# A chain of sigmoid attention and two gated products: layers three and four in four quarters of one form, with a single ScalarE function

## The chip, the core and the metric

The kernel runs on one core of a Trainium2 chip. The metric is device time in microseconds (us), the median of three runs. One further execution was profiled; all rows below come from it.

## The reference, cut to what matters

Four blocks of 448 tokens go through a sigmoid attention (not touched here) and four layers, all in fp32:

```python
x = attention(q, k, v)                                    # 1792 tokens x 768
h = np.maximum(np.maximum(x @ w1, x @ w2), x @ w3)        # layer one, 768 x 768 each
z = h @ moe_w_out                                         # layer two, 768 x 768
h = z @ moe2_w_in                                         # layer three, 768 x 2048
g = h * (1.0 / (1.0 + np.exp(-1.702 * h)))                # the nonlinearity
out = g @ moe2_w_out                                      # layer four, 2048 x 768
```

## The kernel before

**Numbers.** TensorE multiplies in a rounded fp32 format (fp32r). For accuracy every operand is split into a high half (a cast) and a low half (the operand minus its cast), and each product is three matmuls: high by high, high by low, low by high. A cast can go on ScalarE or VectorE (`copy`, L310), a difference only on VectorE (`two`, L313).

**Seven products for eight.** Layers one to three are computed by Strassen's scheme in Winograd's form on blocks of 2 x 2. `moving` makes the seven moving operands from the four blocks of a layer's input (differences, then a high and a low half each, in pieces of 2 x 448 and 448 columns). `Weights` makes the seven stationary operands of a pair of weight tiles: four sums of 128x384 and seven splits, or loads the finished ones from memory (`kept`). A `Set` is one pair of weight tiles over two token blocks: seven products of nine matmuls (L493), and then additions from PSUM that give four tiles of 128x448.

**Layers three and four.** The 1,792 tokens are two pairs of blocks, tp = 1 and tp = 0, and the 2,048 hidden features are 16 tiles, which layer three takes as eight pairs, fp = 0 to 7. A `Group` is one pair for one tp. It runs its Set of layer three; the tiles go through a sigmoid on ScalarE (L828), a multiply and a split on VectorE. Layer four follows directly: `unit` i multiplies the weights of the two feature tiles with the split tiles, six matmuls (L866 to L868), and adds the result on VectorE to the output so far; three of the twelve units keep their PSUM bank from group to group instead. The units of a group are interleaved with the products of the next group's Set. In this way run fp 0 to 3 of tp = 1, then all eight of tp = 0. What is left, fp 4 to 7 of tp = 1, is the last quarter and has a form of its own: its four Sets are staggered by `stage`, and then layer four over all four pairs is done by seven products as well (`Four` splits a moving operand of 4 x 448 columns, `operand4` a weight operand of 128x1536, `combine` and `wide` make the combinations, `product4` at L1008 issues twelve matmuls for each third of the outputs, `finish` adds the first half's result, which was kept in memory as `spill`, and stores). Weights of layer four were split once, kept in memory (`kept4`) and loaded again. The input of layer three is loaded from memory (`reload`) and split again when tp changes.

**The order.** Nothing here is issued as it is written. Each operation is recorded with what it reads and writes, a duration estimate and a due time, and `Order.run` plays the program through once: a free engine takes the ready operation that is due first. The result is a fixed order for each engine, and on the chip each engine goes through its own in that order. `soon` sets a due time a little ahead: with it the conversions of raw 64-bit weights to fp32 (`single`: two instructions on ScalarE, L358 and L363, three on VectorE, one of them L373) are strewn between other work. `prepare` and `prepare4` convert and store a tile for later. All DMAs are issued by one queue, SyncE's.

Of the kernel before, what the change touches and what calls it, by code (L numbers as in the profile page):

```python
# [7 lines left out]
F32 = mybir.dt.float32  # L8
# [178 lines left out]
T = S  # L187
# [6 lines left out]
MW = 15 * T  # L194
NW = 15 * T
FW = 17344
# [7 lines left out]
REDO = (1, 3, 5, 7)  # L204


def moe_chain_kernel(tc, qk, vv, wa, wb, out):
# [20 lines left out]
    sn1, s2, sn2 = Space(NW), Space(MW, gate=lambda: gate["m"]), Space(NW, gate=lambda: gate["n"])  # L228
    sn3, sn4 = Space(8 * T, gate=lambda: gate["n3"]), Space(NW - 8 * T, gate=lambda: gate["n3"])
# [6 lines left out]

    def to_n2(e):
        npool[0].release()
        npool[0] = pool("n2", side="right")
        slab_n.append(npool[0].tile([P, NW], F32R, name="n2"))  # L240
# [7 lines left out]
    def F(at, n):  # L248
        if at >= FAR2:
            return Reg(sn4, at - FAR2, n, lambda: slab_n[3][:, at - FAR2 : at - FAR2 + n])  # L250
# [7 lines left out]
    def R(at, n):  # L258
        if at >= FAR2:
            return Reg(sn3, at - FAR2, n, lambda: slab_n[2][:, at - FAR2 : at - FAR2 + n])  # L260
        if at >= FAR:
            return Reg(sn2, at - FAR, n, lambda: slab_n[1][:, at - FAR : at - FAR + n])
        if at >= RW:
            return Reg(s2, at - RW, n, lambda: slab_m[1][:, at - RW : at - RW + n])
        return Reg(sr, at, n, lambda: slab_r[:, at : at + n])

# [61 lines left out]
    assert y0 + 4 * DM == FW  # L328
# [54 lines left out]
    def split(hi, lo, x, n):  # L383
        copy(hi, x, n)
        sub(lo, x, hi, n)
# [409 lines left out]
    gate["n"] = O.op({"-": 0.0}, to_n2, after=set(sn1.ops))  # L795

    zslots = [slots[i] for i in (1, 2, 3, 4, 5, 6, 0)]
    s3 = 12 * T  # L800
    b3, b4 = Round(range(3)), Round(range(3, 5))
    stay = {2: 5, 6: 6, 10: 7}
    g_at = Round([RW, FAR])
    w4_at = Round([RW + 8 * T + OFF, FAR + 8 * T + OFF, RW + 8 * T + OFF + 2 * DM, FAR + 8 * T + OFF + 2 * DM])
    temp_at.places += [12 * T + 2 * DM + i * T for i in range(2)]
    assert 12 * T + 2 * DM + 2 * T <= tv and 8 * T + OFF + 4 * DM <= min(MW, NW)
    PAIRS = NF // 2

    class Group:


        def __init__(self, fp, tp, z):
            self.fp, self.tp, self.g, self.w = fp, tp, {}, None
            first = self.first = (tp == 1) == (fp < PAIRS // 2)
            early = self.early = fp < EARLY or fp >= PAIRS // 2
            self.set = Set(z, lambda: Weights(12 + fp, first and fp >= READY, s3, early), self.put, b3)
            self.at = None

        def put(self, half, tok, ps, other):
            if self.at is None:  # L820
                self.at = g_at()
            at = self.at + (4 * half + 2 * tok) * T
            if other is not None:
                new = temp()
                add(new, ps, other, S)
                ps = new
# [5 lines left out]
            self.g[half, tok] = hi, lo  # L832

        def weights(self):
            self.w = []
            for half in range(2):
                f, at = self.fp + 8 * half, w4_at()
                hi, lo, both = R(at, DM), R(at + DM, DM), R(at, 2 * DM)
                if self.first:
                    y = F(y_at(), DM)  # L840
                    if self.early:
                        dma(y, y4[f], 384)
                    else:
                        single(wb[tile4(f)], y, "ACT")
                    split(hi, lo, y, DM)
                    if self.fp < PAIRS // 2:
                        dma(kept4[f], both, 768)
                else:
                    dma(both, kept4[f], 768)
                self.w.append((hi, lo))  # L850

        def unit(self, i):
            if self.w is None:
                self.weights()
            tok, o = 1 - i // KC, i % KC
            b = 2 * self.tp + tok
            stays = i in stay
            fresh = not stays or self.fp == 0
            ps, c = banks(stay[i] if stays else b4()), slice(o * P, (o + 1) * P)
            w, g = self.w, [self.g[half, tok] for half in range(2)]  # L860

            def f(_):
                for j in range(2):
                    wh, wl, gh, gl = w[j][0](), w[j][1](), g[j][0](), g[j][1]()
# [275 lines left out]
```

## Time and profile before

| | |
|---|---|
| median of three runs | 866.35 us (865.92 to 868.24) |
| the profiled execution | 865.97 us, its span 864.1 us |
| TensorE (PE) busy | 858.4 us, 99% |
| VectorE (DVE) busy | 684.2 us, 79% |
| ScalarE (ACT) busy | 508.2 us, 59% |
| granted TensorE clock | 1.000 of full speed throughout |
| moved by DMA | 238 MB, mean 276 GB/s |

The span is the time from the first to the last instruction of the program; the execution's time holds some 1.9 us besides. TensorE has two rows in a profile: PE is the matmuls, PEld the weight loads in front of them, which run beside the matmul before. The end of a matmul's record is modelled and reaches past the start of the next, so the rate is read from start to start. The stages of the program follow each other on TensorE: attention to 131.9 us, layers one and two to 434.3, layers three and four to 860.4.

### The profile page before, as it was taken

What the parts mean: (1) busy time and instruction counts of PE and PEld (TensorE: products, weight loads), DVE (VectorE), ACT (ScalarE), POOL (GpSimd) and SP (SyncE); (2) the same over time, 40 slices, a digit from 0 to 9 for tenths busy, and PEclk for the clock granted to TensorE, in tenths of its full rate; (3) what the DMA queues carried; (4) which work ended last, traced back from release to release, by engine and by line L of the source; (5) the groups of instructions that cost most, each with busy time, mean ns of one, the idle gap of its engine ahead of it and who ended that gap; (6) DMA issues with size and microseconds to landing.
All of it is one profiled execution on the core that took longest, in us unless ns stands there. A gap on an engine that the chain in (4) does not pass through costs nothing.

```text
span 864.1 us, 12626 instructions
## 1 busy us (share of the span) xinstructions
PE 858.4 (99%) x4555; PEld 747.8 (87%) x4555; DVE 684.2 (79%) x1096; ACT 508.2 (59%) x743; POOL 0.3 (0%) x5
## 2 busy tenths in 40 slices
PE   9999999999999999999999999999999999999998
PEld 5544548999999999999989999999999999999997
DVE  5898898888898788888597887756696888753894
ACT  7899898565466556667365345655665434423540
POOL 0000000000000000000000000000000000000000
PEclk9999999999999999999999999999999999999999
DMA  8898976877649997899979847988878674786123
GB/s 316 282 369 318 380 264 221 325 243 250 224 170 395 359 378 284 324 333 362 403 295 344 310 144 239 404 317 354 292 237 319 220 258 154 231 281 196 32 64 129
DMA packets 77534, 238.14 MB, mean 276 GB/s; under 512 B 8608, under 2 KB 18208, under 8 KB 77472
## 3 DMA queue, kind: packets, MB, share of 16 engines
q1 hardware_dynamic: 77472, 237.34, 76.7%
q8 instruction: 36, 0.59, 0.3%
q14 instruction: 26, 0.21, 0.1%
HBM read 151.19 MB, written 86.11 MB: 275 GB/s over the span
## 4 chain that ended last, share of the span: by engine, by line
PE 99%; DVE 0%; ACT 0%; issue 0%; DVEq 0%
PE ps L493 58%; PE ps L868 7%; PE ps L610 7%; PE ps L867 7%; PE ps L866 7%; PE ps L1008 6%; PE ps L591 6%; PE ps L654 1%; PE ps L643 1%; PE ps L670 0%; ACT f L310 0%; DVE r L664 0%; DVE n L313 0%; DVEq L1134 0%
## 5 line engine op out<-in xcount | busy, mean ns | idle before, releaser
L493 PE MATMUL ps<-r 128*128 128x448 f32 x2250 | 464.6, 362 | 0.6 <-ACT f L310 0.6
L493 PEld LDWEIGHTS ps<-r 128*128 128x128 f32 x2250 | 421.7, 187 | 29.8 <-ACT f L310 1.0
L313 DVE TENSOR_TENSOR f<-ps,f 128x448 f32<-128x448 f32 x214 | 132.6, 623 | 89.0 <-PE ps L493 27.9
L313 DVE TENSOR_TENSOR r<-f,r 128x384 fp32r<-128x384 f32 (+3 forms) x252 | 161.2, 660 | 17.6 <-ACT r L310 16.3
L310 ACT CAST r<-f 128x384 fp32r<-128x384 f32 (+3 forms) x214 | 120.1, 590 | 44.0 <-PE ps L493 25.2
L310 ACT COPY f<-ps 128x448 f32<-128x448 f32 x128 | 68.8, 541 | 117.7 <-PE ps L493 88.7
L313 DVE TENSOR_TENSOR f<-f 128x384 f32<-128x384 f32 (+2 forms) x189 | 121.4, 660 | 7.8 <-ACT f L929 4.1
L626 ACT ACTIVATE m<-ps,bias 128x896 f32<-128x896 f32 x84 | 79.0, 1006 | 8.6 <-PE ps L591 7.5
L363 ACT ACTIVATE f<-f 128x768 uint8<-128x768 uint32 x38 | 74.8, 1968 | 0.7
L610 PE MATMUL ps<-m,f 128*64 128x448 f32 x288 | 59.4, 548 | 0.0
L493 PE MATMUL ps<-m,r 128*128 128x448 f32 x270 | 57.7, 362 | 0.0
L591 PEld LDWEIGHTS ps<-r 64*128 64x128 f32 x432 | 39.6, 189 | 19.5 <-ACT m L626 9.2
L373 DVE SCALAR_TENSOR_TENSOR f<-f 128x768 uint32<-128x768 uint32 x56 | 53.4, 954 | 1.5 <-ACT f L363 1.1
L493 PEld LDWEIGHTS ps<-m,r 128*128 128x128 f32 x270 | 50.6, 187 | 3.4
L358 ACT ACTIVATE f<-f 128x768 f32<-128x768 f32 x56 | 51.1, 914 | 2.1 <-DMA f<-in_wb 1.0
L591 PE MATMUL ps<-r 64*128 64x448 f32 x432 | 51.3, 379 | 0.0
L610 PEld LDWEIGHTS ps<-m,f 128*64 128x64 f32 x288 | 18.5, 136 | 34.5 <-issue 31.1
L310 ACT COPY ps<-ps 128x448 f32<-128x448 f32 x43 | 22.6, 526 | 38.4 <-PE ps L493 35.3
L310 ACT CAST m<-f 128x448 fp32r<-128x448 f32 (+4 forms) x38 | 27.2, 717 | 30.1 <-DVE f L313 20.5
L313 DVE TENSOR_TENSOR n<-f,n 128x448 fp32r<-128x448 f32 (+4 forms) x51 | 37.8, 747 | 2.4 <-ACT n L310 2.0
L368 DVE TENSOR_SCALAR f<-f 128x768 f32<-128x768 f32 x56 | 31.1, 555 | 9.6 <-ACT f L358 9.5
L313 DVE TENSOR_TENSOR m<-f,m 128x448 fp32r<-128x448 f32 (+4 forms) x41 | 34.0, 833 | 4.7 <-ACT m L310 4.6
(81 smaller groups left out, 883.6 us busy)
## 6 DMA issues: line engine op xcount, KB each, us to landing
r<-kept SPq DMA_DIRECT2D x119, 384.0 KB, 5.9
kept<-r SPq DMA_DIRECT2D x112, 384.0 KB, 5.5
f<-in_wb SPq DMA_DIRECT2D x32, 768.0 KB, 7.2
f<-in_wa SPq DMA_DIRECT2D x24, 768.0 KB, 6.7
f<-yk SPq DMA_DIRECT2D x24, 768.0 KB, 5.6
yk<-f SPq DMA_DIRECT2D x40, 384.0 KB, 5.6
f<-y SPq DMA_DIRECT2D x24, 384.0 KB, 6.0
f<-in_qk SPq DMA_DIRECT2D x15, 456.0 KB, 5.8
```

Of the source, the lines that this page charges most:

```text
L310: return O.op(engines, lambda e: (act.copy if e == "ACT" else dve.tensor_copy)(to(), of()), [of], [to])
L313: return on("DVE", t_two(n), lambda: dve.tensor_tensor(to(), a(), b(), op=op), [a, b], [to])
L363: act.activation(byte(), words(raw(), U32, 0), AF.Copy, scale=LOW)
L373: lambda: dve.scalar_tensor_tensor(u(), words(raw(), U32, 1), 0x80000007, u(), **by),
L493: pe.matmul(o, a[:, c], b, start=fresh and j == n == 0, stop=j == HK - 1 and n == 2, skip_group_check=True,)
L591: pe.matmul(o[:, e, :], kx[r, c * P : (c + 1) * P], qx[r, Q:QK], start=n == 0, stop=n == 2)
L610: pe.matmul(o[r], w[:, 2 * c + e], x[:, e * S : (e + 1) * S], start=begin, stop=end)
L626: lambda: act.activation(a().rearrange("p (e s) -> p e s", e=2), ps(), AF.Sigmoid, bias=bias, scale=scale),
L866: pe.matmul(ps(), wh[:, c], gh, start=fresh and j == 0, **how)
L867: pe.matmul(ps(), wh[:, c], gl, start=False, **how)
L868: pe.matmul(ps(), wl[:, c], gh, start=False, stop=j == 1, skip_group_check=True)
L1008: pe.matmul(o, a, b, start=fresh and k == n == 0, stop=k == 3 and n == 2, skip_group_check=True)
```

## The change

Layers three and four are now run as four quarters, each in the form of the old last quarter: (tp, first or second half of the feature pairs) in the order (1, 0), (0, 0), (0, 1), (1, 1). `Group`, `unit` and `kept4` are gone. A quarter's function runs four Sets staggered by `stage`, loads eight converted weight tiles, and does layer four by seven products, now in the order 0, 2, 1, 3, 4, 5, 6. The first quarter of a tp stores its partial outputs to `spill`, the second adds them and stores the result. The split of a moving operand's high half in `Four` may go only to ScalarE.

The nonlinearity is one ScalarE instruction, `Gelu_apprx_sigmoid`, in place of a sigmoid with scale 1.702 and a multiply.

Layer three's operands of tp = 1 are made once and stored (`zs`); those of tp = 0 are made by `rebuild` from layer two's results, which are loaded into two of the old operand slots; for the last quarter the stored ones are loaded back. In each half, of the pairs in `AGAIN` the stationary operands are made a second time where before all were loaded. The sixteen conversions that before ran with the first four groups of tp = 0 are shared out to the first three quarters (4, 6, 6), and `stage` hands them out in the first 1/1.4 of its steps.

```diff
+AGAIN = (1, 3, 5, 7)
+CONV1, CONV2 = 4, 10
+WITHIN = 1.4
...
-    def stage(sets, extra=()):
+    def stage(sets, extra=(), within=1.0):
...
-            while done * len(steps) < (k + 1) * len(extra):
+            while done < len(extra) and done * len(steps) < (k + 1) * len(extra) * within:
...
-    class Group:
...
-            sg = temp()
-            on("ACT", t_act(S), lambda: act.activation(sg(), ps(), AF.Sigmoid, scale=1.702), [ps], [sg])
-            two(sg, ps, sg, ALU.mult, S)
-            hi, lo = R(at, S), R(at + S, S)
-            split(hi, lo, sg, S)
...
-    def reload(tp):
...
+    def rebuild(old):
+
+        at = old[2:] + old[:2]
+        b = [old[0], old[0] + 3 * T, old[1], old[1] + 3 * T]
+        for i, x in enumerate(b):
+            dma(Z(x, 3 * T), zk[0][i // 2][i % 2][0], 672)
...
+        fill(0, b11)
+        combine(t, b12, b11)
+        fill(1, t)
+        combine(u, b22, t)
+        fill(2, u)
+        combine(t, b21, u)
+        fill(3, b21)
+        combine(u, b22, b12)
+        fill(4, u)
+        fill(5, b22)
+        fill(6, t)
...
-        sg = F(sg_at(), T)
-        on("ACT", t_act(S), lambda: act.activation(sg(), ps(), AF.Sigmoid, scale=1.702), [ps], [sg])
-        two(g, ps, sg, ALU.mult, S)
+        on("ACT", t_act(S), lambda: act.activation(g(), ps(), AF.Gelu_apprx_sigmoid), [ps], [g])
...
+    def quarter(tp, fh, z, extra=(), last=False):
+        again = fh == 1
...
+            i, y = half * fh + k, pair_at()
+            if tp != fh:
+                first = fh == 1 or i >= READY
+            else:
+                first = i in AGAIN
+            return Weights(12 + i, first, s3, y=y, keep=tp != fh and i not in AGAIN)
...
+        four, four_at = Round([FAR2, RING]), Round([*m4, RING + 8 * T + OFF])
+        pa, pb = [], []
+        for n in (0, 2, 1, 3, 4, 5, 6):
...
+    z1 = moving(XA, at=zslots)
+    for k, x in zip(zs, z1):
+        dma(k, R(x.at, SLOT), 1344)
+    quarter(1, 0, z1, convs[:CONV1])
+    z0 = rebuild([x.at for x in z1])
+    quarter(0, 0, z0, convs[CONV1:CONV2])
+    quarter(0, 1, z0, convs[CONV2:])
+    for k, x in zip(zs, z0):
+        dma(R(x.at, SLOT), k, 1344)
+    quarter(1, 1, z0, last=True)
```

In the orders below a row is a run of like instructions: line, operation, destination and source by slab, shape, and how many. f and r are the large slabs (f plain fp32, r fp32r operands), m and n smaller ones with a number behind, ps is PSUM. The changed kernel's lines are one lower than those of before up to layer three, and its own from there.

TensorE at the first entry into layer four, before: units of the first group between products of layer three.

```order
L493 MATMUL ps<-r 128x448 x90
L866 MATMUL ps<-m_1168 128x448
L867 MATMUL ps<-m_1168 128x448
L868 MATMUL ps<-m_1168 128x448
L866 MATMUL ps<-m_1168,n_3522 128x448
L867 MATMUL ps<-m_1168,n_3522 128x448
L868 MATMUL ps<-m_1168,n_3522 128x448
```

The same place after: layer three's products of a whole quarter, then layer four's products n=0 (36), n=2 and n=1.

```order
L492 MATMUL ps<-r 128x448 x261
L909 MATMUL ps<-n_3520,m_1168 128x448 x36
L909 MATMUL ps<-r,m_1168 128x448 x33
L909 MATMUL ps<-n_3520,r 128x448 x3
L909 MATMUL ps<-r,m_1168 128x448 x3
L909 MATMUL ps<-n_3520,r 128x448 x33
L909 MATMUL ps<-r,m_1168 128x448 x33
```

The alternation of units and products is gone; the two layers now follow each other in blocks. In all, TensorE's order has 4,315 matmuls before and 4,207 after.

VectorE in layer four, before (the last quarter, the only one of this form): from the second piece of n=1's low half (951) to the low half for n=3 (957).

```order
L313 TENSOR_TENSOR n_6325<-f,n_6325 128x448
L313 TENSOR_TENSOR m_1168<-f,m_1168 128x1792
L959 TENSOR_TENSOR m_1168<-f,m_1168 128x4x384
L313 TENSOR_TENSOR f<-f 128x1792 x2
L959 TENSOR_TENSOR r<-f,r 128x4x384
L313 TENSOR_TENSOR f<-ps,f 128x448
L313 TENSOR_TENSOR n_6325<-f,n_6325 128x1792
```

VectorE after, first quarter: from the first piece of n=1's low half (128x1344) to the low half for n=3 (the first of 128x1792 into r).

```order
L312 TENSOR_TENSOR n_3520<-f,n_3520 128x1344
L312 TENSOR_TENSOR f<-f 128x1792
L312 TENSOR_TENSOR n_3520<-f,n_3520 128x448
L865 TENSOR_TENSOR m_1168<-f,m_1168 128x4x384
L312 TENSOR_TENSOR f<-f 128x1792
L865 TENSOR_TENSOR f<-f,n_3521 128x4x384
L865 TENSOR_TENSOR m_1168<-f,m_1168 128x4x384
L312 TENSOR_TENSOR r<-f,r 128x1792
```

Product n=2's split has moved out of this stretch to ahead of it, and the weights' work for n=4 (128x4x384, the last two) has come in. A few rows on, still in the first quarter, the rebuilding of layer three's operands (128x896 and 128x448, from and to r) stands between the splits for n=4 and n=5 (the second 128x1792).

```order
L865 TENSOR_TENSOR r<-f,r 128x4x384
L312 TENSOR_TENSOR f<-r 128x896
L312 TENSOR_TENSOR f<-r 128x448
L312 TENSOR_TENSOR n_3521<-r,f 128x896
L312 TENSOR_TENSOR r<-f,r 128x896
L312 TENSOR_TENSOR r<-r 128x896
L312 TENSOR_TENSOR r<-n_3521,r 128x896
L312 TENSOR_TENSOR r<-f,r 128x1792
```

Before, no such work stood in layer four: the operands were made again between two groups.

ScalarE at the first nonlinearity, before (L828 the sigmoid):

```order
L310 CAST r<-f 128x384
L310 CAST r<-f 128x448
L828 ACTIVATE f<-ps 128x448
L310 CAST r<-f 128x896
L310 CAST m_1168<-f 128x448
L310 CAST r<-f 128x448
```

and after (L849):

```order
L309 CAST r<-f 128x896
L362 ACTIVATE f<-f 128x768
L849 ACT_TABLE_LOAD
L849 ACTIVATE f<-ps 128x448
L309 COPY f<-ps 128x448
L309 CAST r<-f 128x384
```

A load of function tables has come in ahead of the first use, the only one besides that at the program's start, and casts of operands stand behind it.

## Rows read from the trace of the kernel before

**Rows 1.** The page: span, and busy us (share) xinstructions of each engine.

```profile
span 864.1 us, 12626 instructions
PE 858.4 (99%) x4555; PEld 747.8 (87%) x4555; DVE 684.2 (79%) x1096; ACT 508.2 (59%) x743; POOL 0.3 (0%) x5
```

**Rows 2.** The page: the chain that ended last, shares of the span by engine.

```profile
PE 99%; DVE 0%; ACT 0%; issue 0%; DVEq 0%
```

**Rows 3.** Waits of the matmuls: us in total, times, longest us.

```profile
PE ps L670 <- DVE r L664: 1.4, 1, 1.4
PE ps L493 <- ACT f L310: 0.6, 1, 0.6
```

**Rows 4.** Timeline of TensorE: start us, us, engine, line, operation, out<-in, count.

```profile
451.53 0.36 PE L866 MATMUL ps<-m 128*128 128x448 f32 x1
451.73 0.36 PE L867 MATMUL ps<-m 128*128 128x448 f32 x1
...
763.05 46.96 PE L493 MATMUL ps<-r 128*128 128x448 f32 x234
809.85 6.76 PE L1008 MATMUL ps<-m 128*128 128x448 f32 x33
```

**Rows 5.** Stretches: length, busy PE, PEld, DVE, ACT, POOL; clock, DMA share, GB/s.

```profile
435.00:451.50 16.50, 15.88 (x79) 14.55 (x79) 16.09 (x28) 11.90 (x23) 0.00 (x0) 1.00 0.71 270
...
763.00:809.90 46.90, 46.90 (x237) 43.95 (x236) 26.34 (x31) 18.52 (x30) 0.00 (x0) 1.00 0.55 168
809.90:861.00 51.10, 50.52 (x253) 47.01 (x251) 40.53 (x42) 17.10 (x19) 0.00 (x0) 1.00 0.28 91
...
434.30:860.40 426.10, 425.48 (x2126) 397.94 (x2124) 320.24 (x495) 207.50 (x318) 0.00 (x0) 1.00 0.69 241
```

**Rows 6.** Groups by shape: busy us, mean ns of one, idle before and its releasers.

```profile
L493 PEld LDWEIGHTS ps<-r 128*128 128x128 f32 x2250 | 421.7, 187 | 29.8 <-ACT f L310 1.0 <-issue 0.7
L313 DVE TENSOR_TENSOR f<-ps,f 128x448 f32<-128x448 f32 x214 | 132.6, 623 | 89.0 <-PE ps L493 27.9 <-PE ps L868 25.3 <-ACT f L828 24.6
L313 DVE TENSOR_TENSOR r<-f,r 128x384 fp32r<-128x384 f32 x168 | 90.2, 554 | 11.7 <-ACT r L310 10.7
L313 DVE TENSOR_TENSOR f<-f 128x896 f32<-128x896 f32 x20 | 21.7, 1086 | 0.1
L313 DVE TENSOR_TENSOR f<-f 128x1344 f32<-128x1344 f32 x2 | 3.1, 1558 | 0.1
L313 DVE TENSOR_TENSOR m<-f,m 128x1792 fp32r<-128x1792 f32 x3 | 6.1, 2022 | 1.3 <-ACT m L310 1.3
L959 DVE TENSOR_TENSOR m<-f,m 128x1536 fp32r<-128x1536 f32 x3 | 5.3, 1751 | 0.0
L373 DVE SCALAR_TENSOR_TENSOR f<-f 128x768 uint32<-128x768 uint32 x56 | 53.4, 954 | 1.5 <-ACT f L363 1.1
L310 ACT CAST m<-f 128x1792 fp32r<-128x1792 f32 x2 | 3.4, 1697 | 7.9 <-PE ps L1008 7.9
L828 ACT ACTIVATE f<-ps 128x448 f32<-128x448 f32 x24 | 13.1, 544 | 34.4 <-PE ps L493 34.4
L322 ACT ACT_TABLE_LOAD x1 | 1.3, 1283 | 0.7 <-PEq L1126 0.7
```

**Rows 7.** Timelines of VectorE, ScalarE and TensorE in the last quarter's layer four.

```profile
829.20 2.02 DVE L313 TENSOR_TENSOR n<-f,n 128x1792 fp32r<-128x1792 f32 x1
831.13 1.15 DVE L313 TENSOR_TENSOR f<-ps,f 128x448 f32<-128x448 f32 x2
...
831.65 1.70 ACT L310 CAST m<-f 128x1792 fp32r<-128x1792 f32 x1 [2.78 <-PE ps L1008]
...
831.45 6.76 PE L1008 MATMUL ps<-n,m 128*128 128x448 f32 x33
```

**Rows 8.** DMA: packets and mean rate; loads of layer-two results, median us to landing.

```profile
DMA packets 77534, 238.14 MB, mean 276 GB/s; under 512 B 8608, under 2 KB 18208, under 8 KB 77472
...
f<-z SPq DMA_DIRECT2D x8, 672.0 KB, 6.5
```

More of the change, by code (lines that the diff above doesn't have):

```diff
@@ L794, in moe_chain_kernel @@
     layer2(h, False, XA)
-    gate["n"] = O.op({"-": 0.0}, to_n2, after=set(sn1.ops))
+    gate["n"] = O.op({"-": 0.0}, to_n3, after=set(sn1.ops))
+    half = NF // 4
     zslots = [slots[i] for i in (1, 2, 3, 4, 5, 6, 0)]
     s3 = 12 * T
[L801 to L805, printed above, removed]
@@ L806, in moe_chain_kernel @@
-    assert 12 * T + 2 * DM + 2 * T <= tv and 8 * T + OFF + 4 * DM <= min(MW, NW)
-    PAIRS = NF // 2
-    class Group:
[L812 to L826, printed above, removed]
-            sg = temp()
-            on("ACT", t_act(S), lambda: act.activation(sg(), ps(), AF.Sigmoid, scale=1.702), [ps], [sg])
-            two(sg, ps, sg, ALU.mult, S)
-            hi, lo = R(at, S), R(at + S, S)
-            split(hi, lo, sg, S)
[L832 to L864, printed above, removed]
-                    how = dict(stop=False, skip_group_check=True)
-                    pe.matmul(ps(), wh[:, c], gh, start=fresh and j == 0, **how)
-                    pe.matmul(ps(), wh[:, c], gl, start=False, **how)
-                    pe.matmul(ps(), wl[:, c], gh, start=False, stop=j == 1, skip_group_check=True)
-            O.pe(f, 6 * MM, [y for z in (*w, *g) for y in z] + ([] if fresh else [ps]), [ps])
-            at = (tok * KC + o) * T
-            done = self.fp == (PAIRS // 2 if self.tp else PAIRS) - 1
-            if stays and not done:
-                return
-            a = F(at, T)
-            if self.fp == 0 or stays:
-                copy(a, ps, S, psum=True)
-            else:
-                add(a, ps, a, S)
-            if done and self.tp:
-                dma(spill[tok * KC + o], a, 224)
-            elif done:
-                O.op({"SP": 224 / BUS}, lambda e: sp.dma_start(out[o, :, b * S : (b + 1) * S], a()), [a], [])
@@ L913, in moe_chain_kernel @@
-    z = reload(1)
-    for i in range(2 * KC):
-        before.unit(i)
-    gate["n3"] = O.op({"-": 0.0}, to_n3, after=set(sn2.ops))
-    places = [16 * T + i * T for i in range(9)]
-    assert places[-1] + T <= raw0 and 8 * DM == FW - raw0
-    bank_at = Round([0, 1, 2, 5, 6, 7, 3, 4])
-    mu_at, sg_at = Round(places[:5]), Round(places[5:])
-    G = [4 * i * T for i in range(4)]
+    G = [0, 4 * T, 8 * T, 12 * T + 4 * HW]
+    places = [G[3] + (4 + i) * T for i in range(5)]
+    a2_at, acc0 = FAR2, FAR2 + 4 * HW
@@ L1010, in product4, with finish @@
             O.pe(f, 3 * MM, [w[0][k], w[1][k], hi, lo] + ([] if fresh and k == 0 else [ps]), [ps])
[L1012 to L1014 removed]
+    u2, m5 = [F(a, T) for a in places[:3]], [F(a, T) for a in (*places[3:], FW - T)]
     late = ((0, 3), (3, 1))
[L1017 to L1020 removed]
+    def finish(tp, again, at, side, tok, i, ps, other=None, last=False):
+        o, b = i + 3 * side, 2 * tp + tok
+        at += i * T
+        a, kept = F(at, T), spill[tp][tok * KC + o]
+        if not again:
+            if other is None:
+                copy(a, ps, S, psum=True)
+            else:
+                add(a, ps, other, S)
+            dma(kept, a, 224)
+            return
+        dma(a, kept, 224)
         if other is not None:
[L1022 removed]
+            add(a, other, a, S)
         for h in [slice(0, S // 2), slice(S // 2, S)] if last else [slice(0, S)]:
```

189 lines of the change are left out of this document (85 added, 104 removed).

## The prediction

> **What bounds the kernel now.** I read the page's totals first, then the chain, then who made TensorE wait, and only then single rows. TensorE is busy 858.4 of 864.1 us [rows 1] and is 99% of the chain that ended last [rows 2]. The waits of TensorE are the view that decides: after the warm-up it lost 0.6 us, once, in the whole program [rows 3]. The stretch that the change rewrites, layers three and four, lasts from 434.3 to 860.4 us: 426.1 us, of which TensorE is busy 425.5 [rows 5]. It is a plain queue of matmuls. One starts every 0.200 us, whichever loop issued it: the 234 of layer three from 763.05 to 809.85 us are 46.80 us, and in the direct layer four the L867 starts 0.20 us after the L866 [rows 4]. 2,124 matmuls by 0.200 are 424.8 us of the 426.1. So the time of this stretch is a count, as long as VectorE, ScalarE and the DMA queue deliver operands in time. VectorE is busy 320.2 of the 426.1 us there and ScalarE 207.5 [rows 5].
>
> That gives one price for a removed matmul, and there is a second: its weight load takes 187 ns [rows 6]. If a removed matmul gave back only that, 108 of them would be 20.2 us and the time 846.7 us. The Trainium skill, "Perfetto Trace Analysis", section "Identifying the Most-Contended Engine", calls matmul busy time a bad measure and judges by the weight loads' share, 87% here [rows 1], which speaks for the second price. The start-to-start rows say 0.200, and I go by them.
>
> **What is removed.** Layer three keeps its matmuls: 16 sets of seven products of nine, 1,008. Layer four loses some. Before, three quarters go direct: twelve pairs of tiles, twelve units each, six matmuls a unit, 864; the last quarter goes by seven products, 7 x 3 x 4 x 3 = 252. After, all four go by seven products, 1,008. That is 1,116 - 1,008 = 108 matmuls, and all before layer three is the same on TensorE. 108 x 0.200 = **21.6 us**, on the engine that sets the end. The stretch becomes 2,016 x 0.200 = 403.2 us, four quarters of 100.8, half of each layer three and half layer four.
>
> Removed on VectorE: the multiply behind each sigmoid (64 by about 0.62 us [rows 6]) and most additions that collected layer four from PSUM. Cost or gain on the path: nothing, since TensorE did not wait for them [rows 3].
>
> **What is added, and what hides it.** The last quarter of before is the new form already, so it is the template. There layer three and then layer four ran without a gap on TensorE, with VectorE busy 26.3 of 46.9 and 40.5 of 51.1 us [rows 5]. The three new quarters carry more, so I add VectorE up for the first, the fullest one, from [rows 6]. Layer three: eight additions from PSUM, 8 x 0.62 = 5.0. Layer four: seven low halves of the moving operand, 7 x 2.02 = 14.2; seven of the weights, 7 x 1.75 = 12.3; four combinations of weights, 7.0, and four of moving operands, 8.1; six additions, 3.7. This base is 50.3. On top: three sets whose weights are made anew, each seven low halves and four sums of 0.55, 18.3; four conversions of a raw weight tile, three instructions of at most 0.95 each, 11.4; and the rebuilding of layer three's operands for the other two token blocks, seven low halves and five differences, each in pieces of 896 and 448, 12 x (1.09 + 0.62) = 20.5. Sum 100.5 us, against 100.8. But records overlap: a 2.02 us instruction gives way to the next after 1.93 [rows 7], 0.09 less, and some 110 instructions make that 9.9 us. So 90.6 of 100.8 us, 90%. VectorE did better than that without hurting: 16.1 of 16.5 us at the start of layer three, at the price of the one 0.6 us wait [rows 3, 5]. The others have less: quarter two base plus two sets and six conversions, 50.3 + 12.2 + 17.1 = 79.6; quarter three twelve further additions for the second pass, four sets, six conversions, 50.3 + 7.5 + 24.4 + 17.1 = 99.3 before overlap; quarter four 70.0.
>
> Sums do not show order, so I follow the two tightest places. **First, the seam from quarter one to two.** The rebuilding stands between the splits of layer four, and its last low half stands in VectorE's order between the second and the third addition of layer four's product n=5. The three additions of n=4 are done when that product ends, 36 us into layer four; from there to the end of the rebuilding the order holds about 22 us of records, some 20 us in time, so it ends near 57. Layer three's set 0 is interleaved with set 1, so its seventh product comes after nine others, at 50.4 + 16.2 = 66.6 us. Cover 9 us: price 0. Its four loads of 672 KB land in 6.5 us each [rows 8], in the two slots that the last set of layer three gives up first; they are wanted only in the second half of layer four. **Second, the product n=3 of layer four.** Products come in the order 0, 2, 1, 3, each 36 matmuls, 7.2 us, so n=3 is due at 21.6. The moving operand has two places, so the split for n=1 waits until product 0 has left its place, as the cast at 831.65 waited for TensorE [rows 7], and reaches VectorE at about 8.5. From there to the end of n=3's low half the order holds 1.56 + 2.02 + 0.62 + 1.75 + 2.02 + 1.75 + 1.75 + 2.02 = 13.5, less 8 x 0.09: 12.8, so 21.3 in quarter one, and with one more small piece 21.9 in quarter two, 0.3 late plus the handing over. I take 0.5 us there, bounds 0 and 2 (the two 1.75 in front of it). In quarters three and four the order has fewer ahead.
>
> **ScalarE.** One function replaces sigmoid and multiply. Its duration is not in the trace; the sigmoid took 0.544 us on the same shape [rows 6]. At twice that, all 64 would be 35 us more on an engine idle for half of this stretch; I take 0.544, price 0. The order shows one more table load, in front of the first use, in quarter one's set 0; the one of before took 1.283 us [rows 6]. Queued behind it are casts for the rebuilt operands and weights. Before, the seven products of set 0 ran back to back and the wait was 0.6; now the last operand is due 5.4 us later. I take 0, bounds 0 and 1.3.
>
> The Trainium skill, "ScalarE: Activation LUTs", section "What ACT_TABLE_LOAD costs", gives 1283 ns for the load, which the row agrees with, and 1380 ns of drain besides, which no run here shows; by 2.66 us the upper bound would be 2.7.
>
> **DMA.** From the issues with their sizes: the direct layer four's kept weights and 28 kept operands each way go (12.6 + 22 MB), and so do four loads of layer-two results (2.8); saved operands of layer three out and in (19.3), more partial sums (5.5), weight tiles that are read again (3.1 + 3.1) come. 237 MB become 231, so the queue has less to do than at the mean of 276 GB/s [rows 8]. Price 0.
>
> **The sum.** The profiled execution took 865.97 us, its span 864.1. Span: 864.1 - 21.6 + 0.5 = 843.0, plus the 1.9 around it 844.9. The median of before lies 0.4 above that execution: **845.3 us**.
>
> **Rivals.** (1) *The two places of the moving operand become a chain.* Each split is a ScalarE cast of 1.70 and a VectorE half of 2.02 inside a window of 7.2 us, behind whatever else is queued. For: n=3 is at its limit by my own sum. Against: in the template the half at 829.20 ended at 831.22, 0.2 us before its product began at 831.45, and nothing was lost [rows 7]. If each of three full quarters loses 1 to 2 us at two products, 2 to 6 us in all: 847.5 to 851. (2) *VectorE cannot be filled.* In layer four of the template it was busy 79% (40.5 of 51.1), its gaps being waits for TensorE and ScalarE. If 79% is its ceiling, quarter one's 90.6 us take 114.3, and quarter three's 99.3, less 10.3 for overlap, take 112.2: 13.5 + 11.4 = 25 us over. That eats the gain: 870, **slower**. It decides when the two overruns pass 24.2 us (gain plus 2.6). Against it: 97% at the start of layer three [rows 5], and the template had nothing to fill its gaps with. (3) *Half of that*, one of the two quarters over, by 9 to 14 us: 854 to 859. That the change doesn't do what it says I give nothing: TensorE's order holds 4,207 matmuls for 4,315.
>
> **Chances.** Forecast, 843.8 to 847.5: 0.66. Rival 1, up to 851: 0.21. Rival 3: 0.08. Rival 2: 0.03 slower, and 0.02 for overruns that land within 0.3% (2.6 us, about what a measurement of this kernel can tell from no change). The range takes the forecast and rival 1. Its low end is the count alone with the old 0.6 us wait gone and 0.4 us of spread between runs, 843.8; its high end 851. The second price of a matmul (846.7) has a tenth, inside the forecast's share. Faster 0.95, same 0.02, slower 0.03.
>
> **What would show it.** The matmuls of the new line for layer four at 0.200 us; layers three and four together 403 to 405 us long; TensorE's waits in that stretch under 2 us, the largest at product n=3 of quarter one or two, ended by VectorE. Rival 1 shows as waits of about 1 us for VectorE's halves at many products, rivals 2 and 3 as waits around 535 us and 735 us with VectorE above 95%. I am wrong if the new function is far slower than the sigmoid, or if a late DMA landing stops VectorE in order.

## The result, and the profile after

The changed kernel takes **843.32 us** (843.07 to 844.5), the kernel before, measured beside it, 866.42 (865.92 to 868.24): a ratio of 0.9732 (0.9716 to 0.9749), 23.1 us less. The forecast was 845.3 with a range of 843.8 to 851.0. The sign and nearly all of the size were right; the time lies 2.0 us under the forecast and 0.5 us below the range. The profiled execution of the changed kernel is the slowest of the four, 844.5 us with a span of 842.7, so a second profile of the same kernel, of an execution of 842.94 us, is used beside it. It is called a_same below.

The page of the changed kernel, first its totals (busy us, share, instructions), then the chain's shares and the DMA line; these answer to [rows 1, 2, 8]:

```profile
span 842.7 us, 12281 instructions
PE 836.4 (99%) x4447; PEld 726.2 (86%) x4447; DVE 697.3 (83%) x1009; ACT 538.7 (64%) x756; POOL 0.3 (0%) x5
...
DMA packets 73788, 231.83 MB, mean 275 GB/s; under 512 B 8192, under 2 KB 20864, under 8 KB 71936
...
PE 29%; DVE 2%; DMA 1%; issue 0%; ACT 0%; SPq 0%; DVEq 0%
```

108 matmuls are gone from the PE row (4,555 to 4,447) and PE is busy 22.0 us less. VectorE, which lost the multiplies, is busy 13 us more than in [rows 1]. The chain of 29% TensorE looks alarming beside the 99% of [rows 2], and is not: followed backward, it leaves TensorE at one wait of 0.43 us, goes through a load and breaks off at 566.7 us, so it leaves out all that TensorE did before. The waits show how little that was. The matmuls' waits, us in total, times, longest, in the profiled execution and, in the second block, in a_same (they answer to [rows 3]; L590 and L669 are before layer three):

```profile
PE ps L669 <- DVE r L663: 1.4, 1, 1.4
PE ps L590 <- DVE r L309: 1.1, 1, 1.1
PE ps L909 <- DVE r L312: 0.4, 1, 0.4
```

```profile
PE ps L669 <- DVE r L663: 1.4, 1, 1.4
PE ps L590 <- DVE r L309: 0.5, 1, 0.5
```

So a_same has no wait in layers three and four large enough for this view, and the 0.6 us of [rows 3] is gone in both. The four quarters in the profiled execution, then the two halves of quarter one (layer three, layer four); columns as in [rows 5]:

```profile
434.87:535.70 100.83, 100.83 (x506) 94.41 (x505) 93.66 (x117) 71.85 (x103) 0.00 (x0) 1.00 0.75 285
535.70:637.40 101.70, 101.27 (x505) 94.33 (x504) 85.30 (x108) 65.80 (x91) 0.00 (x0) 1.00 0.61 217
637.40:738.30 100.90, 100.90 (x505) 94.44 (x505) 84.29 (x107) 60.17 (x83) 0.00 (x0) 1.00 0.90 337
738.30:839.10 100.80, 100.80 (x505) 94.31 (x503) 67.46 (x74) 36.89 (x55) 0.00 (x0) 1.00 0.32 109
...
434.87:485.27 50.40, 50.40 (x254) 47.24 (x252) 44.25 (x71) 36.34 (x60) 0.00 (x0) 1.00 1.00 383
485.27:535.70 50.43, 50.43 (x254) 47.17 (x253) 49.40 (x47) 35.51 (x43) 0.00 (x0) 1.00 0.50 187
```

The quarters sum to 404.2 us; the count alone is 403.2 (2,016 by 0.200). Quarter one's layer four is the place to look at: VectorE is busy 49.40 of 50.43 us, 98%, and TensorE runs through it without a gap.

The only real loss, 0.9 us, is in quarter two. The chain of the profiled execution shows where it came from (start us, us, what):

```profile
570.00 8.85 DMA f<-y
...
578.93 1.56 DVE f L865
...
592.02 2.02 DVE r L312
594.05 0.04 issue
594.09 43.49 PE ps L909 x215
```

A raw weight tile of 384 KB (y) took 8.85 us to land where the median was 6.9. The weights' combination that needs it stood at the head of VectorE's queue, and all behind it came late. So the low half for n=2 began only at 592.02 (590.53 in a_same), and TensorE stood for 0.43 us, 0.7 us counted from start to start. The other 0.2 us are at n=3. In a_same this load was in time and the wait did not occur. These two stretches, layers three and four (0.8 us) and attention (0.8 us, 0.6 of it the longer wait at L590, 1.1 for 0.5 us), are the 1.6 us between the two profiles.

### The profile page after: what moved, and what is told of

Same layout as the page of the kernel before. It is cut to its first block, busy times and chain, and to the rows that moved or that the text cites. A ratio compares the mean times of both kernels' runs of the same rounds, so it can differ in the third digit from the quotient of the medians.

```text
span 842.7 us, 12281 instructions
## 1 busy us (share of the span) xinstructions
PE 836.4 (99%) x4447; PEld 726.2 (86%) x4447; DVE 697.3 (83%) x1009; ACT 538.7 (64%) x756; POOL 0.3 (0%) x5
## 5 line engine op out<-in xcount | busy, mean ns | idle before, releaser
L492 PE MATMUL ps<-r 128*128 128x448 f32 x2250 | 454.6, 362 | 0.0
L312 DVE TENSOR_TENSOR r<-f,r 128x384 fp32r<-128x384 f32 (+4 forms) x235 | 163.0, 711 | 24.3 <-ACT r L309 22.7
L309 ACT CAST r<-f 128x384 fp32r<-128x384 f32 (+4 forms) x199 | 124.2, 649 | 45.3 <-PE ps L492 22.4
L312 DVE TENSOR_TENSOR f<-f 128x384 f32<-128x384 f32 (+4 forms) x140 | 103.5, 759 | 5.7 <-ACT f L849 4.7
L312 DVE TENSOR_TENSOR f<-ps,f 128x448 f32<-128x448 f32 (+1 forms) x117 | 71.6, 616 | 42.2 <-PE ps L492 31.2
L909 PE MATMUL ps<-n,m 128*128 128x448 f32 x432 | 90.8, 362 | 0.0
L909 PEld LDWEIGHTS ps<-n,m 128*128 128x128 f32 x432 | 81.0, 188 | 5.4
L909 PE MATMUL ps<-r,m 128*128 128x448 f32 x288 | 61.4, 363 | 0.4 <-DVE r L312 0.4
L909 PEld LDWEIGHTS ps<-r,m 128*128 128x128 f32 x288 | 53.8, 188 | 4.8 <-DVE r L312 1.1
L590 PEld LDWEIGHTS ps<-r 64*128 64x128 f32 x432 | 38.4, 184 | 21.1 <-ACT m L625 9.5
L590 PE MATMUL ps<-r 64*128 64x448 f32 x432 | 50.7, 374 | 1.1 <-DVE r L309 1.1
L312 DVE TENSOR_TENSOR r<-n,r 128x384 fp32r<-128x384 f32 (+3 forms) x65 | 46.5, 724 | 3.2 <-ACT r L309 2.5
```

The lines of the kernel that those rows point to most:

```text
L309: return O.op(engines, lambda e: (act.copy if e == "ACT" else dve.tensor_copy)(to(), of()), [of], [to])
L312: return on("DVE", t_two(n), lambda: dve.tensor_tensor(to(), a(), b(), op=op), [a, b], [to])
L492: pe.matmul(o, a[:, c], b, start=fresh and j == n == 0, stop=j == HK - 1 and n == 2, skip_group_check=True,)
L590: pe.matmul(o[:, e, :], kx[r, c * P : (c + 1) * P], qx[r, Q:QK], start=n == 0, stop=n == 2)
L909: pe.matmul(o, a, b, start=fresh and k == n == 0, stop=k == 3 and n == 2, skip_group_check=True)
```

## The experiments

Every variant is planned again by the same program, so an edit that adds or removes work also moves other instructions. No run holds the order fixed: the price of an edit below is that of the work together with the order that the planner then makes. The diffs are against the changed kernel unless said. The kernel before, measured beside a_same, b_same, b_gelu and a_sigmoid, took 866.64 us (865.78 to 868.22), beside the others, which ran on other chips, 866.51. Differences from a_same across chips can be off by about that 0.1 us.

**a_same: the changed kernel again.** No edit.

> The changed kernel once more, unaltered, for a second profile and more times. Its first profile was of the slowest of four executions (844.50 us, the others 843.07 to 843.44). Theory A: 1.1 us of that is a wait in the attention stage that most executions don't have, and up to 0.6 us a wait in quarter two's layer four; a new profile at 843.1 to 843.5 us then shows layers one and two beginning near 131.9 us instead of 132.35, and layers three and four 403.2 to 403.8 us long instead of 404.2. Rival B: the executions differ in layers three and four, by waits of VectorE and DMA that come and go: the start of layer one stays at 132.3 and the stretch differs by 1 us or more.

Measured: 843.07 us (842.94 to 843.94), ratio 0.973 (0.9717 to 0.9744). Layers three and four in this profile, and the halves of VectorE and TensorE around n=3 of quarter one:

```profile
434.50:838.00 403.50, 403.20 (x2015) 377.19 (x2013) 330.85 (x403) 234.27 (x330) 0.00 (x0) 1.00 0.65 238
```

```profile
502.45 1.76 DVE L865 TENSOR_TENSOR m<-f,m 128x1536 fp32r<-128x1536 f32 x1
504.12 2.02 DVE L312 TENSOR_TENSOR r<-f,r 128x1792 fp32r<-128x1792 f32 x1
506.09 0.96 DVE L879 CAST r<-f 128x1536 fp32r<-128x1536 f32 x1
```

```profile
484.49 7.36 PE L909 MATMUL ps<-n,m 128*128 128x448 f32 x36
...
499.49 6.76 PE L909 MATMUL ps<-n,r 128*128 128x448 f32 x33
506.09 6.78 PE L909 MATMUL ps<-r,m 128*128 128x448 f32 x33
```

The low half for n=3 (504.12) ends at 506.14. Its product begins at 506.09, 21.60 us into layer four, and its second matmul, at 506.30, is the first that reads the low half. That leaves at most 0.2 us of slack.

**b_same, b_same2, b_same3: the kernel before again,** to see whether its old waits stand in every execution and where its spread goes. No edit.

> The kernel before once more, unaltered, for a second profile. Its first profile (865.97 us) lost about 1.0 us between matmuls in layers three and four: 0.8 us at 443 us and 0.2 us at 759 us. Theory A: these two are part of the planned order and stand in every execution, 0.6 to 1.1 us at the same two places; then the new form gains them on top of the 21.6 us. Rival B: they come and go, and a second profile shows less than 0.3 us; then what is over 21.6 us is only the spread between executions.

> The kernel before again, for a third profile. Its two profiled executions (865.97 and 865.71 us) lie at the low end of its times (865.8 to 868.2, median 866.6). Theory A: a slower execution has the same waits of 1.0 us in layers three and four and loses more ahead of them, in the attention stage. Rival B: the waits at 443 us grow.

> As b_same2, for a fourth profile: where an execution above 866 us loses its time.

Measured: 865.71, 866.06 and 866.02 us. All three have the old wait: TensorE's matmuls of set 0 in the first of them (start us, us, count, idle before):

```profile
440.82 2.57 PE L493 MATMUL ps<-r 128*128 128x448 f32 x12
444.01 2.28 PE L493 MATMUL ps<-r 128*128 128x448 f32 x10 [0.62 <-ACT f L310]
```

From start to start it costs 0.8 us, and 0.1 more at a matmul just behind it. The second, small one near 759 us comes and goes: 0.11 us in the first profile of before, 0.06 in b_same, none in the other two. So theory A holds for the wait at 444 us alone. b_same2 and b_same3 start layer one some 0.2 us later than the first profile of before (a wait of attention's, 1.0 and 0.5 us long). All three are in the lower half of before's spread. What makes its executions of 867 and 868 us longer was not caught and stays open.

**b_gelu: the kernel before, with the one function in both places,** and nothing else of the change:

```diff
-            on("ACT", t_act(S), lambda: act.activation(sg(), ps(), AF.Sigmoid, scale=1.702), [ps], [sg])
-            two(sg, ps, sg, ALU.mult, S)
+            on("ACT", t_act(S), lambda: act.activation(sg(), ps(), AF.Gelu_apprx_sigmoid), [ps], [sg])
```

> The kernel before with the one function in place of sigmoid and multiply, all else as it was. Theory A (TensorE never waited for the multiply): within 0.6 us of before, 865.7 to 866.9 us; the table load of 1.3 us falls at the first use near 441 us, where TensorE already waits 0.6 us, and may lengthen that wait by up to 1.3 us. Rival B: the function takes longer than the sigmoid's 0.54 us and shows as waits for ScalarE: 868 us or more.

Measured: 865.36 us (864.84 to 866.46), ratio 0.9987 (0.9978 to 0.9996): 1.3 us less, between 0.3 and 1.9. The wait at 444 us is gone, as TensorE's timeline at the same place shows:

```profile
440.71 5.56 PE L493 MATMUL ps<-r 128*128 128x448 f32 x27
```

VectorE's busy time in layers three and four falls from 320.2 to 293.6 us. So taking the multiplies out is enough to lose the old wait. That they were part of a crowd of VectorE and ScalarE work at the start of layer three fits this, but the run also reorders that work. By the profiles, 0.9 us of the 1.3 are in layers three and four (424.9 us for 425.8 in b_same); the rest isn't placed.

**a_sigmoid: the changed kernel with sigmoid and multiply,** all else of the change kept:

```diff
-        on("ACT", t_act(S), lambda: act.activation(g(), ps(), AF.Gelu_apprx_sigmoid), [ps], [g])
+        on("ACT", t_act(S), lambda: act.activation(g(), ps(), AF.Sigmoid, scale=1.702), [ps], [g])
+        two(g, ps, g, ALU.mult, S)
```

> The changed kernel with the sigmoid (scale 1.702) and the multiply on VectorE in place of the one function: 64 multiplies of about 0.54 us start to start, 8.6 us more for VectorE in each quarter, and no second table load. Theory A (VectorE is nearly full in quarter one, 93.7 of 100.8 us, and has room elsewhere): quarter one comes to 102 us of work, its waits 1 to 4 us, the rest free: 844 to 848 us. Rival B (cover is ample, the one function is worth nothing): 843 to 844 us. Rival C (VectorE can't be filled, every full quarter overruns): 850 us or more.

Measured: 862.71 us (860.7 to 864.85), ratio 0.9955 (0.9938 to 0.9973). Nearly the whole gain is lost, 19.6 us. The matmuls' waits, then TensorE in quarter one, then two stretches (columns as in [rows 5]):

```profile
PE ps L910 <- DVE n L312: 4.8, 3, 3.0
PE ps L910 <- ACT n L309: 3.6, 2, 1.8
PE ps L910 <- DVE r L312: 3.5, 3, 1.9
```

```profile
433.69 51.76 PE L492 MATMUL ps<-r 128*128 128x448 f32 x258
...
500.23 5.77 PE L910 MATMUL ps<-n,r 128*128 128x448 f32 x28
506.20 1.88 PE L910 MATMUL ps<-n,r 128*128 128x448 f32 x8 [0.21 <-DVE n L312]
509.85 0.55 PE L910 MATMUL ps<-n,m 128*128 128x448 f32 x1 [1.78 <-ACT n L309]
513.41 4.09 PE L910 MATMUL ps<-n,m 128*128 128x448 f32 x11 [3.00 <-DVE n L312]
```

```profile
485.76:544.30 58.54, 53.30 (x254) 48.45 (x253) 56.72 (x54) 38.91 (x46) 0.00 (x0) 0.94 0.44 169
...
513.40:517.30 3.90, 3.89 (x11) 3.49 (x12) 3.90 (x3) 0.00 (x0) 0.00 (x0) 0.55 0.00 0
```

The waits stand where the moving operand changes after n=1, some 20 us into layer four, in quarters one, two and three; quarter four has none. The late starts sum to 18.0 us of the 18.6 by which the span is longer than a_same's. They hold two parts. TensorE waits, and after two of the long waits it is slow: most of the eleven matmuls of the last row start 0.373 us apart, at a granted clock of 0.55, close to the lower of TensorE's two levels (1.2 of 2.4 GHz). 3.4 of the 18.0 us are that. 64 multiplies, some 31 us of VectorE's time over four quarters (361.4 against 330.9 us), with the order that they bring, thus cost 19.6 us here and 1.3 in the old form. The first row shows one thing more: layer three of quarter one runs from 433.69 us without a gap, multiplies and all. The old wait at 444 us is gone here too, so the new form loses it by itself.

**a_more: one more matmul for every third,** 252 in all, in layer four; they repeat one that stands there already:

```diff
+                    if k and not n:
+                        pe.matmul(o, a, b, start=False, stop=False, skip_group_check=True)
...
-            O.pe(f, 3 * MM, [w[0][k], w[1][k], hi, lo] + ([] if fresh and k == 0 else [ps]), [ps])
+            O.pe(f, (4 if k else 3) * MM, [w[0][k], w[1][k], hi, lo] + ([] if fresh and k == 0 else [ps]), [ps])
```

> The changed kernel with 252 matmuls more: in layer four each unit of three matmuls but the first of a chain of four repeats its first one, so the output is no longer the reference's. It prices a matmul. Theory A (TensorE is a queue of matmuls at 0.200 us): +50.4 us on 843.1, 893.3 to 893.7 us. Rival B (a matmul costs its weight load, 0.187): +47.1, 890.2. Rival C (the changed kernel waits for VectorE in places, which more matmuls would cover): less than 50 us, by as much as the waits were, 0.3 us or more below A.

Measured: 893.36 us (893.15 to 893.99), 50.3 us more than a_same: 0.1996 us for each matmul. At 0.187, the weight load, it would have been 47.1. No wait in layers three and four.

**a_dummy: 80 subtractions of 128x336 on spare columns,** five behind every set of layer three, due 8 us later:

```diff
+        for _ in range(2 if (half, tok) == (1, 0) else 1):
+            O.op(
+                {"DVE": t_two(SPARE)},
+                lambda _: dve.tensor_tensor(spare(), Z(WREG + NWS * WSLOT, SPARE)(), spare(), op=ALU.subtract),
+                [spare],
+                [spare],
+                after=[o],
+                at=O.clock + 8.0,
+            )
```

> The changed kernel (with its one function) plus VectorE work that nothing waits for: behind each set's tiles five subtractions of 128x336 on a spare place, 80 in all, due 8 us after the tile. Some 0.42 us each start to start, 34 us, as much as the 64 multiplies of the sigmoid form. Theory A (the multiplies cost 19.6 us because they stand in the chain between the tile and its split, at a seam where VectorE has no gap): work that may be put off fills VectorE's gaps, 843 to 847 us. Rival B (VectorE has no capacity left, whatever the place): 858 to 866 us, as with the multiplies.

Measured: 858.95 us (857.73 to 859.4), 15.9 us more than a_same. TensorE and VectorE at n=3 of quarter one:

```profile
507.99 0.47 PE L921 MATMUL ps<-r,m 128*128 128x448 f32 x1 [0.58 <-ACT r L309]
511.48 4.88 PE L921 MATMUL ps<-r,m 128*128 128x448 f32 x16 [3.01 <-DVE r L312]
```

```profile
506.07 3.42 DVE L877 TENSOR_TENSOR m<-f,m 128x1536 fp32r<-128x1536 f32 x2
509.41 2.02 DVE L312 TENSOR_TENSOR r<-f,r 128x1792 fp32r<-128x1792 f32 x1
```

The half for n=3, at 504.12 in a_same, starts at 509.41. Five of the added rows, 2.1 us from start to start, stand on VectorE between 484 and 496 us; the rest of the delay is other work of the same queue that the new order puts in front of it, two weights' halves (506.07) among it. The same happens in quarters two and three. Here the multiplies' place in the chain can't be the reason, as theory A had it: nothing waits for the added work. Alone, this time looks as if VectorE were simply full. The next run asks whether it is the amount or the place.

**a_early: the same 80 subtractions, elsewhere:** only behind the first two sets of layer three, none in quarter one, 16, 16 and 48 in the others.

```diff
-        for _ in range(2 if (half, tok) == (1, 0) else 1):
+        for _ in range({(1, 0): 0, (0, 0): 2, (0, 1): 2, (1, 1): 6}[now[-1]] if k < 2 else 0):
```

> The same 80 VectorE subtractions of 128x336 as in the run a_dummy, 34 us in all, now only behind the first two sets of layer three: none in quarter one, 16 each in quarters two and three, 48 in quarter four, so that they are over before the seam into layer four. Theory A (what costs is VectorE work in the 25 us around the seam, up to product n=3, and not the sum): 843 to 845 us. Rival B (VectorE's sum is what counts, as 80 of them at every set cost 15.9 us): 855 us or more.

Measured: 847.98 us (847.75 to 849.65), 4.9 us more than a_same instead of 15.9. 4.6 of the 4.9 stand at n=3 of quarter two. The stretches of quarter two's layer four and of quarter four's layer three read:

```profile
586.30:640.00 53.70, 51.21 (x247) 47.28 (x246) 45.87 (x48) 30.96 (x38) 0.00 (x0) 0.97 0.40 130
...
738.00:788.50 50.50, 50.50 (x254) 47.34 (x254) 44.83 (x73) 21.97 (x40) 0.00 (x0) 1.00 0.43 147
```

48 subtractions in quarter four cost nothing, though VectorE is busy 44.83 of 50.50 us there. In quarter two 16 of them cost 4.9 us with VectorE at 85%. In quarter three another 16 cost some 0.1 us. So neither the total nor a quarter's share of busy time decides. The result lies between the two theories, nearer to the one of the place, and the place is not that of the added rows themselves: in quarter two the last of them ends at 571.6 us, some 15 us before layer four begins. What is late there is work that they pushed back, and in the new order a cast of 0.95 us (at 607.45) stands on VectorE in front of the half for n=3, where a_same has it behind. How much of the 4.6 us is the one and how much the other is not shown. That what counts is the queue in front of n=3 fits both runs; no run varies that alone.

**a_order: layer four's products in the order 0, 1, 2, 3** as in the kernel before, in place of 0, 2, 1, 3:

```diff
-        for n in (0, 2, 1, 3, 4, 5, 6):
+        for n in range(7):
```

> The changed kernel with layer four's products in the old order 0, 1, 2, 3, 4, 5, 6 in place of 0, 2, 1, 3, 4, 5, 6. Product n=1 needs two combinations of moving operands and two of weights before its splits, and is now due 7.2 us after the start of layer four instead of 14.4. Theory A (VectorE is without a gap at the start of layer four in the three full quarters): n=1 comes 1 to 4 us late in each, 846 to 855 us. Rival B (that order had no wait in the old last quarter, and has none here): 843 to 844 us.

Measured: 850.44 us (848.46 to 850.65), 7.4 us more. TensorE and the wait at n=3 of quarter one:

```profile
508.44 0.37 PE L909 MATMUL ps<-r,m 128*128 128x448 f32 x1
510.05 2.27 PE L909 MATMUL ps<-r,m 128*128 128x448 f32 x10 [1.25 <-DVE r L312]
```

Late starts at n=3 of quarters one to three cost 1.5, 1.5 and 2.6 us, 5.6 in all; n=1, which theory A had expected late, was in time. The rest stands in attention, which ends 2.3 us later in this execution than in a_same (1.0 of it a longer wait at L590) and which the edit does not touch. So the new order of products is worth some 5 to 6 us, and the prediction gave it no number.

**a_load: no stationary operand of layer three is made a second time;** all are loaded, as before the change:

```diff
-AGAIN = (1, 3, 5, 7)
+AGAIN = ()
```

> The changed kernel with AGAIN empty: the stationary operands of all pairs are kept in memory and loaded the second time, none is made twice. VectorE loses four sets of eleven instructions, some 21 us, in quarters two and four; DMA gets some 19 MB more, writes in quarters one and three, where the DMA engines are at a share of 1.00 in layer three, and reads in two and four. Theory A (making them again is hidden): no time to gain, 843 to 844 us, unless the DMA runs over. Rival B (DMA is at its limit there): 5.5 MB more in layer three of quarters one and three are 14 us each at 383 GB/s, and as waits for loads behind them 846 us or more.

Measured: 855.01 us (853.26 to 855.65), 11.9 us more, with less work on VectorE. First the first loads of quarter two's weights (y) in the queue's order, in a_same and, behind the dots, here; then quarter two's layer three, then VectorE and TensorE at n=3 of quarter two:

```profile
556.73 0.32 SPq L294 DMA_DIRECT2D f<-y  x1
...
566.98 1.00 SPq L294 DMA_DIRECT2D f<-y  x2
```

```profile
536.40:587.00 50.60, 50.55 (x253) 47.06 (x252) 23.77 (x33) 27.32 (x39) 0.00 (x0) 1.00 0.94 362
```

```profile
606.70 3.43 DVE L865 TENSOR_TENSOR m<-f,m 128x1536 fp32r<-128x1536 f32 x2 [0.38 <-ACT m L879]
610.05 2.02 DVE L312 TENSOR_TENSOR r<-f,r 128x1792 fp32r<-128x1792 f32 x1
```

```profile
612.12 6.07 PE L909 MATMUL ps<-r,m 128*128 128x448 f32 x29 [2.91 <-DVE r L312]
```

VectorE idles more than half of that layer three, mostly because it has less to do: 23.77 us for 39.6 in the same half of a_same, of which some 12 are the two sets that are not made again. The loads of y are issued from 567.0 us on instead of 556.7, behind the added loads, with the DMA engines at 0.94 for 0.79, and the first combination of weights starts at 583.3 for 577.5 in a_same. Then the work that was not done early stands in front of n=3's half. No computing engine is seen waiting for y in this quarter, so the delay lies in the planned order. That the planner put it there for the later loads is inferred; no run moved y alone.

**a_norebuild: the operands of layer three are not rebuilt;** quarters two to four use those of tp = 1, so the loads, seven low halves and five differences drop out.

```diff
-    z0 = rebuild([x.at for x in z1])
+    z0 = z1
```

> The changed kernel without the rebuilding: quarter two and three use quarter one's operands of layer three, so the output is not the reference's. VectorE and ScalarE lose 24 instructions each and the queue four loads, all in quarter one's layer four. Theory A (the rebuilding is hidden, price 0): 842.8 to 843.3 us. Rival B (it delays product n=3 or the first products of quarter two): 842.5 us or less.

Measured: 843.38 us (843.15 to 844.25), ratio 0.9732 (0.9717 to 0.9746), equal to a_same within the spread, although VectorE has 13.7 us less to do. Layers three and four last 403.2 us by the starts of their matmuls, 0.2 less than in a_same: the small loss at n=3 of quarter two is gone. The rebuilding is hidden but for at most that.

## Why the prediction came out as it did

**The count: right.** 108 by 0.200 = 21.6 us. Layers three and four last 404.2 us in one profile and 403.5 in the other, with 403.2 predicted for the matmuls, and a_more gives 0.1996 us for a matmul more. The second price falls with it: the Trainium skill, "Perfetto Trace Analysis", section "Identifying the Most-Contended Engine", would judge TensorE's headroom by the weight loads' share, besides the useful arithmetic done (86% of the span here, 93% of layers three and four). The headroom that this leaves was not there: a matmul more costs its whole 0.200.

**"Cost or gain on the path: nothing": the step that failed, and the sum with it.** This was said of the multiplies, from the one wait of 0.6 us, and the sum then took off the 21.6 us of the count and nothing else: it carried the waits of before into the new form. Both were wrong. The multiplies had a price: 1.3 us in the old form (b_gelu, which loses the old wait) and 19.6 us in the new one (a_sigmoid). And the old wait did not belong in the sum: it is gone in a_same, and it is gone in a_sigmoid too, which keeps the multiplies, so the new form's order is enough to lose it, as the multiplies' removal is in the old form. The prediction had a reason for that, the last operand of set 0 due 5.4 us later, and used it only for the low end. I had even noted that 424.8 of the 426.1 us were matmuls and left the rest in the sum. By the profiles of b_same and a_same, 863.85 and 841.14 us, the 22.7 us are: 21.6 the count, 0.74 waits of layers three and four (1.0 before, 0.2 after), 0.26 a shorter end (4.06 us from the last matmul's start to the end of the span before, 3.80 after; not foreseen), 0.13 attention's waits. My sum took only the first, and added 0.5 for n=3. The span forecast of 843.0 is 1.9 above a_same's: 0.5 + 0.74 + 0.26 + 0.13, and 0.25 by which the profiled execution of before was longer than b_same.

**"The median lies 0.4 above that execution": a wrong carry-over.** That is how far before's median lay above its profiled execution. The changed kernel's a_same runs lie within 0.2 us of each other with one exception at 843.94, so the median is 0.1 above the profiled one. That is another 0.3 us, and with it the 2.2 us between the forecast and a_same's 843.07; the first measurement, 843.32, lies 0.2 above that by its spread. The low end was built with the same errors: it allowed 1.0 us beside the count (one old wait of 0.6 us, 0.4 us of spread), and the medians 866.35 and 843.32 differ by 1.4 beside it. What the low end lacked is mostly the shorter end (0.26) and 0.14 more of waits. Of the forecast's 2.2 us, the waits of layers three and four and the 0.5 for n=3 are the largest part, 1.24.

**VectorE's sums: somewhat low, harmless.** With the overlap of quarter one on all four (a tenth), the sums were 90.6, 71.8, 89.0 and 63.1, in all 314 us; measured were 93.7, 85.3, 84.3 and 67.5, 330.7. I had put every cast on ScalarE. 21 of them, 13.5 us, ran on VectorE. A part of quarter one's rebuilding also fell into quarter two.

**The seam: right.** The last piece of the rebuilding ended some 59 us into layer four (57 predicted, 66.6 due), and a_norebuild confirms the price of 0.

**Product n=3: right, within 0.3 us.** The half was to end 21.3 us into layer four of quarter one and 0.3 late in quarter two; it ended 21.6 in quarter one, and quarter two lost 0.2. The 0.5 in the sum was too much by 0.3. The place was right, the reason only in part: in quarter two of a_same the half waited 0.17 us for its cast on ScalarE, which stood behind a copy from PSUM, and not for VectorE's queue alone.

**ScalarE: right.** The new function takes what the sigmoid took on the same shape [rows 6], and the load of its table what the other load took. The groups, and ScalarE around the load:

```profile
L849 ACT ACTIVATE f<-ps 128x448 f32<-128x448 f32 x32 | 17.4, 544 | 17.3 <-PE ps L492 17.2
...
L849 ACT ACT_TABLE_LOAD x1 | 1.3, 1283 | 0.0
```

```profile
446.58 1.96 ACT L362 ACTIVATE f<-f 128x768 uint8<-128x768 uint32 x1
448.56 1.28 ACT L849 ACT_TABLE_LOAD   x1
449.85 0.55 ACT L849 ACTIVATE f<-ps 128x448 f32<-128x448 f32 x1
```

The load starts 0.02 us after the instruction before it and the function follows at once. The Trainium skill, "ScalarE: Activation LUTs", section "What ACT_TABLE_LOAD costs", has 1380 ns of drain besides; this trace has no idle time there for it, and TensorE did not wait.

**DMA: right on the total** (231.8 MB; the text starts from 237 where [rows 8] has 238.1), blind to the peaks: the share is 1.00 in layer three of quarter one. That there is little to spare fits a_load and the one late y of the profiled execution, though in a_load no wait at n=3 was one for a load. "A late DMA landing stops VectorE in order" was named as a way to be wrong; it cost 0.7 us, once.

**The rivals.** Rival 2's ceiling of 79% falls: VectorE ran at 98% for 50 us with no loss. Rival 1's mechanism, the operand for n=3 coming late, cost 0.2 us in the change, but it is what the disturbances that cost time set off: a_sigmoid, a_dummy, a_early, a_order and a_load lose most of their 5 to 20 us at n=3 or at its neighbours. The forecast was right about which of the two would be the case. What my text did not say is how near the edge this is, and that the one function, which it priced at nothing, is part of what keeps the change from it.

## What to carry to other kernels

Where TensorE is one unbroken queue, price removed matmuls by their start-to-start time, and then list every gap that is left in the stretch and ask of each whether the change keeps its cause; a small old wait is not a constant. An edit that takes work off an engine that hardly anybody waits for was worth 1.3 us in the old form and 19.6 in the new one, so price it in both. A busy share over a quarter does not tell whether an engine in strict order keeps up: add up what stands in its queue from a seam to the first operand that is wanted.

## What the runs showed of the hardware

A wait can cost more than its length. After some of the waits (3.0 us behind another of 1.8 at 513 us in a_sigmoid, 3.0 behind 0.6 in a_dummy, 1.6 behind 0.4 at 716 us in a_load) the next six to fifteen matmuls started 0.373 us apart instead of 0.200, with a granted clock of 0.55 in that stretch of a_sigmoid, and then went back to 0.200. Such runs of slow matmuls are 3.4 us of a_sigmoid's loss. Length alone does not tell which waits are followed by one: a_load stood 2.9 us at 612 us and a_order 2.3 us at 716 us, and both went on at full pace. The Trainium skill, "TensorE: Matmul & The Clock Gate", section "Wait — 56ns, not 53.3ns?", gives the columns divided by 1.2 GHz as the pace at the lower level; the estimate from that is 373 ns for 448 columns, which this agrees with.
